# Loading w1 of the later experts as four transfers of 32 rows each

## The chip, the core and the metric

The kernel runs on one core of a Trainium2 chip. The metric is the device time of one execution in microseconds; the time before is 1105.34 us, the median of three runs (1098.51 to 1108.52).

## The reference

Windowed attention (8 batches, 8 heads, 576 positions, head size 64; half the heads plain, half dilated) feeds a mixture of experts over its 4608 rows of 512:

```python
top2 = np.argpartition(-noisy_logits, 2, axis=1)[:, :2]
...
for e in range(E):                              # E = 8
    for k in range(2):
        mask = top2[:, k] == e
        h = np.maximum(x[mask] @ w1[e], 0.0)    # w1[e]: 512 x 1024
        out[mask] += top2_w[mask, k, None] * (h @ w2[e])   # w2[e]: 1024 x 512
```

All is float32.

## The kernel before

The program has two stages. Up to about 240 us it computes attention and the gate, writes the attention's rows to a scratch tensor in DRAM (`xs`) and a table of (row, weight) entries per expert (`tab`). From then on it works through the eight experts. Expert 0 is fixed; the order of the other seven is found at run time, so their weights are read at an address that is held in a register (`EID`, `row`, lines 681 to 687).

An expert's tokens are at most 1152 to 1216, in three blocks of 3, 4 and 2 or 3 tiles of 128 tokens. For a block, `up` (line 811) runs 8 x 12 matmuls into PSUM buffers named `up`, and for each of the eight f ScalarE (ACT) takes the relu into `hh` (line 827) and VectorE (DVE) the rest into `hl` (line 829). `down` (line 877) then runs 24 matmuls per tile into one of two PSUM buffers named `dn` (line 865); DVE scales the result into `y` (line 874) and GpSimd (POOL) scatters it with an add into the output (line 842). Each float32 operand is held as a high and a low part, and three products of parts replace one product.

w1 of an expert comes in four chunks `kc` of 128 rows x 1024, 512 KB each. `stage_w1` (line 692) has SyncE (SP) issue the load into a buffer `ws`, and `split_w1` (line 699) has ACT cast it into `w1h` (line 703) and DVE subtract into `w1l` (line 705). The pool of `ws` has two buffers, shared with the loads of w2 (line 709). So the loads of chunks 2 and 3 are issued only when DVE has taken chunks 0 and 1, which it does after the last `up` of the expert before. Meanwhile PE runs four tiles of `down`, and then needs the new w1.

In the later experts the rows of a chunk are not contiguous in DRAM. The tokens' rows are gathered in pieces of 128 columns and transposed in blocks of 32 x 32, so that partition 32 q + d of chunk c stands for column 128 q + 32 c + d. The load of chunk kc therefore takes four blocks of 32 rows, 128 rows apart, one for each quadrant q of the partitions.

Each engine executes its own instructions in the order of the program. That order is made by a list of due times (`plan` and `tick`, lines 893 to 904) that is kept in units of PE's work; it decides between which matmuls a load, cast or gather is written. The order on SP's queue is the order of issue: the index loads of a later expert (lines 744, 747, 749: `ixt`, `ixs`) and the loads of w2 stand behind the loads of w1.

Of the kernel before, what the change touches and what calls it, by code (L numbers as in the profile page):

```python
# [46 lines left out]
def attention_moe_kernel(ctx, tc, qt, kp, kd, vpl, vdl, w_gate, w_noise, noise, w1, w2, out, CAPS=(1216, 1216, 1216, 1184, 1184, 1152, 1152, 1152), SPLITS=(0, 384, 896)):  # L47
    nc = tc.nc
    tensor, vector, scalar, gpsimd, sync = nc.tensor, nc.vector, nc.scalar, nc.gpsimd, nc.sync
# [636 lines left out]
    def row(w, e):  # L686
        return w[e] if isinstance(e, int) else w[bass.ds(e, 1)].rearrange("o a b -> (o a) b")
# [4 lines left out]
    def stage_w1(e, kc):  # L692

        s = late["stage"].tile([128, FF], F32, name="ws", tag="ws")
        sync.dma_start(s, w1[0][128 * kc:128 * kc + 128] if type(e) is int else
                       row(w1, e).rearrange("(q c d) f -> c q d f", q=4, c=4)[kc])
        ST[1, kc] = s

    def split_w1(kc):
# [292 lines left out]
    for kc in range(4):  # L992
        a, b = ((-3, 2), (-2, 3), (4, 6), (5, 7))[kc]
        at(L0 + SL_W1 + a, lambda kc=kc: stage_w1(0, kc))
        at(L0 + SL_W1 + b, lambda kc=kc: late.__setitem__(("w", kc), split_w1(kc)))
        at(L0 + SL_W1 + b + 1, lambda kc=kc: late.pop(("w", kc))())
# [78 lines left out]
    for e in range(E):  # L1075
# [50 lines left out]
        if not last:  # L1126
            t = start + (42 if first else 20)
            plan(t, lambda e=e: (new_idx(e + 1), idx_dma(e + 1, 0, CAPS[e + 1])))
            t = max(t + (14 if first else 9), at_[0, 1])
            plan(t - 0.5, lambda e=e: idx_copy(e + 1, 0, CAPS[e + 1]))  # L1130
            plan_x(e + 1, 0, t, *((6, 13) if first else (9, LAG)))
            plan_x(e + 1, 1, t + (18 if first else 27), *((6, 12) if first else (9, LAG)))
            t = at_[0, 2] + dur(e, 2, False)
            plan(t - 8, lambda e=e: (stage_w1(EID[e + 1], 0), stage_w1(EID[e + 1], 1)))
            for c in range(4):
                plan(t + 0.5 + 3 * c, lambda c=c: split_w1(c), 1.2)
                if c < 2:
                    plan(t + 0.6 + 3 * c, lambda c=c, e=e: stage_w1(EID[e + 1], c + 2))
# [15 lines left out]
    with tc.If(big > 0):  # L1154
        with tc.For_i(0, E, 1) as r:
            e = nc.values_load(ci[0:1, bass.ds(r, 1)], min_val=0, max_val=E - 1)
# [74 lines left out]
```

## Time and profile before

| | |
|---|---|
| runs | 1098.51, 1105.34, 1108.52 us |
| the profiled execution | 1100.93 us |
| its span, first to last instruction | 1099.3 us |
| mean granted TensorE clock | 0.962 |
| busy: PE, POOL, DVE, ACT | 93%, 48%, 42%, 29% of the span |
| loads of w1 and w2 on SP's queue (`ws`) | 64, 512 KB each |
| mean DMA rate over the span | 121 GB/s |

PE is the TensorE matmul queue, PEld its weight loads. A row "ACT w1h L703 <- DMA ws<-in_moe_w: 109.7, 13, 11.2" reads: ACT stood idle before the instructions of line 703 that write w1h until a DMA that writes ws had landed, 109.7 us in all, 13 times, 11.2 us the longest. Times in the timeline count from the first instruction. A granted clock of 1.00 is TensorE's full clock.

### The profile page before, as it was taken

Reading aid. Unit: us, or ns where it says so; the run is one execution under the profiler, and the core shown is the slowest. Engines: PE = TensorE matmul, PEld = TensorE weight load, DVE = VectorE, ACT = ScalarE, POOL = GpSimd, SP = SyncE. Lnnn points to the kernel's source line nnn. Section 1 sums busy time; section 2 is a strip of 40 time slices with the busy share of each in tenths; the row PEclk is TensorE's granted clock in tenths of the full one; section 3 lists DMA queues with packets and bytes.
Section 4 is the critical chain, followed back from the end, with each engine's and each line's share of the span. In section 5 each row is a group of like instructions: output and inputs, shape, how many; then the busy total and the mean of one; then the engine's idle time right before and its main releaser. Section 6 shows DMA issues by size and latency. Waiting matters only on the chain. (4 is left out here: it accounts for less than half of the span.)

```text
span 1099.3 us, 18395 instructions
## 1 busy us (share of the span) xinstructions
PE 1020.7 (93%) x7274; PEld 856.7 (78%) x7275; DVE 463.2 (42%) x1060; ACT 318.2 (29%) x609; POOL 528.2 (48%) x727
## 2 busy tenths in 40 slices
PE   7997767679999999999999999999999999999996
PEld 4774645567787889978987889788878888888885
DVE  7673636545133544344344333433453334333221
ACT  6673535531112322232223122312231222222110
POOL 7004243555767455655544554465445555653112
PEclk9997988889999999999999999999999999999998
DMA  8899587465235243443444334334333533353123
GB/s 282 309 336 296 151 276 259 150 198 145 47 88 122 74 98 61 118 89 82 79 95 84 89 78 97 88 79 86 79 94 71 124 50 107 64 127 60 32 29 46
DMA packets 77530, 132.91 MB, mean 121 GB/s; under 512 B 29968, under 2 KB 39616, under 8 KB 76160
## 3 DMA queue, kind: packets, MB, share of 16 engines
q1 hardware_dynamic: 55088, 92.55, 26.5%
q0 software_dynamic: 22352, 39.15, 19.9%
q8 instruction: 58, 0.95, 0.4%
q14 instruction: 32, 0.26, 0.1%
HBM read 92.11 MB, written 39.54 MB: 120 GB/s over the span
## 5 line engine op out<-in xcount | busy, mean ns | idle before, releaser
L823 PE MATMUL up<-x,w1h 128*128 128x512 f32 (+4 forms) x1536 | 398.7, 345 | 12.4 <-DVE hl L829 7.8
L823 PEld LDWEIGHTS up<-x,w1h 128*128 128x128 f32 x1536 | 273.9, 190 | 41.0 <-DVE hl L829 9.4
L775 POOL DMA_INDIRECT g<-xs,ixi x258 | 265.2, 1028 | 84.2 <-issue 78.9
L823 PE MATMUL up<-x,w1l 128*128 128x384 f32 (+4 forms) x768 | 264.6, 344 | 0.8 <-DVE w1l L705 0.8
L865 PE MATMUL dn<-w2h,hh 128*128 128x512 f32 x576 | 227.2, 394 | 4.5 <-DVE y L874 3.6
L865 PE MATMUL dn<-w2h,hl 128*128 128x512 f32 x576 | 225.5, 392 | 1.8 <-issue 1.7
L865 PE MATMUL dn<-w2l,hh 128*128 128x512 f32 x576 | 225.4, 391 | 0.2 <-issue 0.2
L829 DVE SCALAR_TENSOR_TENSOR hl<-up,hh 128x384 fp32r<-128x384 f32 (+2 forms) x192 | 106.0, 556 | 231.0 <-ACT hh L827 176.7
L842 POOL DMA_INDIRECT out_rows<-y,ixs x67 | 107.4, 1603 | 189.8 <-DVE y L874 161.0
L827 ACT ACTIVATE hh<-up 128x384 fp32r<-128x384 f32 (+4 forms) x192 | 94.2, 498 | 264.1 <-PE up L823 205.7
L823 PEld LDWEIGHTS up<-x,w1l 128*128 128x128 f32 x768 | 145.9, 190 | 13.2 <-DVE w1l L705 1.4
L865 PEld LDWEIGHTS dn<-w2h,hh 128*128 128x128 f32 x576 | 108.9, 189 | 29.7 <-DVE y L874 5.9
L865 PEld LDWEIGHTS dn<-w2h,hl 128*128 128x128 f32 x576 | 108.8, 189 | 24.8 <-issue 1.8
L865 PEld LDWEIGHTS dn<-w2l,hh 128*128 128x128 f32 x576 | 109.0, 189 | 22.5 <-issue 0.6
L874 DVE TENSOR_SCALAR y<-dn,ixs 128x512 f32<-128x512 f32 x63 | 46.9, 748 | 145.1 <-PE dn L865 120.7
L794 ACT CAST x<-xr 128x512 fp32r<-128x512 f32 x67 | 40.5, 604 | 188.9 <-DVE xr L792 160.8
L628 POOL DMA_INDIRECT tab<-en,si x72 | 71.1, 988 | 34.8 <-issue 16.1
L705 DVE TENSOR_TENSOR w1l<-ws,w1h 128x1024 fp32r<-128x1024 f32 x32 | 38.8, 1219 | 96.0 <-ACT w1h L703 88.9
L306 POOL COPY spacer<-hh 1x1 f32<-1x1 f32 x72 | 24.2, 336 | 99.5 <-ACT hh L827 99.2
L703 ACT CAST w1h<-ws 128x1024 fp32r<-128x1024 f32 x32 | 33.0, 1047 | 117.8 <-DMA ws<-in_moe_w 109.7
L795 DVE TENSOR_TENSOR x<-xr,x 128x512 fp32r<-128x512 f32 x67 | 44.6, 666 | 18.0 <-ACT x L794 15.2
L792 DVE STREAM_TRANSPOSE xr<-g 128x512 f32<-128x512 f32 x67 | 45.7, 682 | 0.0
(186 smaller groups left out, 859.5 us busy)
## 6 DMA issues: line engine op xcount, KB each, us to landing
ws<-in_moe_w SPq DMA_DIRECT2D x64, 512.0 KB
out_rows<-zero SPq DMA_DIRECT2D x38, 256.0 KB
vd<-in_vdl SPq DMA_DIRECT2D x24, 390.0 KB
vp<-in_vpl SPq DMA_DIRECT2D x16, 585.0 KB
qt<-in_qt SPq DMA_DIRECT2D x14, 576.0 KB
xs<-x SPq DMA_DIRECT2D x24, 256.0 KB
kt<-in_kd SPq DMA_DIRECT2D x16, 320.0 KB
g<-xs,ixi POOLq DMA_INDIRECT x258
```

Source lines behind the costliest of these rows:

```text
L628: ins = gpsimd.indirect_dma_start(out=tab, out_offset=bass.IndirectOffsetOnAxis(ap=si[:, kq, t:t + 1], axis=0), in_=en[:, kq, t], in_offse ...
L705: return lambda: vector.tensor_tensor(b, s, a.bitcast(F32), op=OP.subtract)
L775: gpsimd.indirect_dma_start(out=g[:, j], out_offset=None, in_=xq, in_offset=bass.IndirectOffsetOnAxis(ap=IX[e][1][:, r0 // 32 + j:r0 // 32 ...
L792: vector.transpose(xr[:, :, 0:rn].rearrange("p c (g t) -> p g c t", t=32), g[:, 0:n].rearrange("p g (c d) -> p g c d", d=32))
L794: scalar.copy(xh[:, :, o:o + rn], xr[:, :, 0:rn])
L795: return lambda: vector.tensor_tensor(xl[:, :, o:o + rn], xr[:, :, 0:rn], xh[:, :, o:o + rn].bitcast(F32), op=OP.subtract)
L823: tensor.matmul(p[:, 0:n], lhsT=a[:, 128 * f:128 * f + 128], rhs=b[:, kc, 0:n], start=(i == 0), stop=(i == 11))
L827: scalar.activation(hh[:, f, 0:n], p[:, 0:n], AF.Relu)
L829: vector.scalar_tensor_tensor(hl[:, f, 0:m], p[:, 0:m], 0.0, hh[:, f, 0:m].bitcast(F32), op0=OP.max, op1=OP.subtract)
L842: ins = gpsimd.indirect_dma_start(out=out, out_offset=bass.IndirectOffsetOnAxis(ap=sc[0:rn, t, 1:2], axis=0), in_=y[0:rn], in_offset=None, ...
L865: tensor.matmul(p[0:rn], lhsT=a[:, f, o:o + rn], rhs=b[:, f % 2], start=(i == 0), stop=(i == 23))
L874: vector.tensor_scalar(y[0:rn], p[0:rn], wsc, None, op0=OP.mult)
```

## The change

Where the expert's number is only known at run time, the one transfer of 128 rows becomes four of 32 rows, one for each quadrant of the partitions. The same rows go to the same partitions. Expert 0 keeps its load of 128 contiguous rows.

```diff
     def stage_w1(e, kc):
 
         s = late["stage"].tile([128, FF], F32, name="ws", tag="ws")
-        sync.dma_start(s, w1[0][128 * kc:128 * kc + 128] if type(e) is int else
-                       row(w1, e).rearrange("(q c d) f -> c q d f", q=4, c=4)[kc])
+        if type(e) is int:
+            sync.dma_start(s, w1[0][128 * kc:128 * kc + 128])
+        else:
+            for q in range(4):
+                sync.dma_start(s[32 * q:32 * q + 32], row(w1, e)[128 * q + 32 * kc:128 * q + 32 * kc + 32])
         ST[1, kc] = s
```

Seven experts with four chunks each make 28 loads before and 112 transfers now. A loop at the end of the program, for experts with more tokens than planned, holds 4 loads more, which become 16; it is not entered with these inputs. The order of PE, ACT, DVE and POOL stays as it was; only SP has more instructions (525 rows where it had 333).

SP, the loads of chunks 2 and 3 of the fourth expert that runs, and the index loads behind them. `ws_5882` and `ws_5907` are the two buffers; DMAHW is a hardware DMA semaphore, of which there are eight in turn. Before:

```order
L695 DMA ws_5882<-in_moe_w1 128x1x1024 [waits DMAHW5_49,DMAHW3_49,DVE_49]
L695 ISA
L695 DMA ws_5907<-in_moe_w1 128x1x1024 [waits DMAHW6_49,DMAHW4_49,DVE_49]
L744 ISA
L744 DMA ixt_6197<-tab_58 32x37x2 [waits Pool_49]
L747 ISA
```

The same place now (each of the two loads has four transfers with an ISA row ahead of each; rows that repeat are left out):

```order
L699 DMA ws_5912<-in_moe_w1 32x1024 [waits DMAHW5_49,DMAHW4_49,DMAHW6_49,DMAHW3_49,DVE_49]
L699 ISA
L699 DMA ws_5912<-in_moe_w1 32x1024
...
L699 DMA ws_5940<-in_moe_w1 32x1024 [waits DMAHW2_49,DMAHW1_49,DMAHW7_49,DMAHW0_49,DVE_49]
...
L747 ISA
L747 DMA ixt_6233<-tab_58 32x37x2 [waits DMAHW3_49,Pool_49]
L750 ISA
```

The first transfer of each load waits for DVE and for the four transfers that filled the buffer last; the other three wait for nothing more. The index load that stood behind two issues stands behind eight.

ACT, the casts of that expert's w1. Before:

```order
L703 CAST w1h1_5904<-ws_5800 128x1024 [waits DMAHW4_49]
L703 CAST w1h2_5940<-ws_5882 128x1024 [waits DMAHW5_49]
L703 CAST w1h3_5956<-ws_5907 128x1024 [waits DMAHW6_49]
L794 CAST x_5670<-xr_5966 128x4x128 [waits DVE_49]
L794 CAST x_5670<-xr_6022 128x4x128 [waits DVE_49]
L827 ACTIVATE hh_6032<-up_6034 128x384 [waits PE_49,Activation_49,Pool_49]
```

Now:

```order
L706 CAST w1h1_5937<-ws_5827 128x1024 [waits DMAHW2_49,DMAHW7_49,DMAHW1_49,DMAHW0_49]
L706 CAST w1h2_5976<-ws_5912 128x1024 [waits DMAHW5_49,DMAHW6_49,DMAHW4_49,DMAHW3_49]
L706 CAST w1h3_5992<-ws_5940 128x1024 [waits DMAHW2_49,DMAHW7_49,DMAHW1_49,DMAHW0_49]
L797 CAST x_5694<-xr_6002 128x4x128 [waits DVE_49]
L797 CAST x_5694<-xr_6058 128x4x128 [waits DVE_49]
L830 ACTIVATE hh_6068<-up_6070 128x384 [waits PE_49,Activation_49,Pool_49]
```

Nothing has moved; a cast waits for four semaphores where it waited for one, and the casts of x and the relus of the next `up` stand behind it as before.

## The prediction

> **What bounds the kernel now.** I read the busy table first, then one window over the expert stage, then who waits for whom in it.
>
> ```profile
> PE 1020.7 (93%) x7274; PEld 856.7 (78%) x7275; DVE 463.2 (42%) x1060; ACT 318.2 (29%) x609; POOL 528.2 (48%) x727
> 300.00:1099.00 799.00, 779.18 (x3854) 669.64 (x3853) 305.09 (x491) 183.72 (x310) 403.72 (x501) 0.99 0.39 83
> ```
>
> The second row is the stretch in which all seven later experts run; its columns after the length are the busy times of PE, PEld, DVE, ACT and POOL, the granted clock, the share of the 16 DMA engines and GB/s. PE is busy 779.2 of 799 us. So whatever faster loads do for the other engines, the kernel gains only what PE loses by waiting. These are PE's waits in that stretch, all of them:
>
> ```profile
> PE dn L865 <- DVE y L874: 3.6, 3, 2.1
> PE up L823 <- DVE hl L829: 2.6, 4, 1.0
> PE dn L865 <- issue: 2.2, 3, 1.7
> PE up L823 <- ACT w1h L703: 1.6, 1, 1.6
> PE up L823 <- DVE w1l L705: 0.8, 2, 0.6
> PE up L823 <- issue: 0.5, 1, 0.5
> PE dn L859 <- DVE y L874: 0.4, 1, 0.4
> ```
>
> The columns are microseconds in total, how often, and the longest. The sum is 11.7 us. Only 2.4 us names w1 outright, so the question is what stands behind DVE's lateness in the rows on y and hl. The engines' own longest waits in the same stretch point at it:
>
> ```profile
> ACT w1h L703 <- DMA ws<-in_moe_w: 109.7, 13, 11.2
> DVE w1l L705 <- ACT w1h L703: 88.9, 17, 8.7
> ```
>
> Thirteen times ACT stands before a cast of w1 until its load lands, up to 11.2 us, and DVE stands behind ACT. One such place, the w1 load of the fourth expert that runs, in the timeline (start, length, engine, line, in brackets the idle time before and its cause):
>
> ```profile
> 538.16 2.35 SPq L695 DMA_DIRECT2D ws<-in_moe_w  x2
> ...
> 543.67 9.34 SPq L747 DMA_DIRECT2D ixs<-tab  x1
> ...
> 549.86 1.05 ACT L703 CAST w1h<-ws 128x1024 fp32r<-128x1024 f32 x1 [11.22 <-DMA ws<-in_moe_w]
> 556.45 1.05 ACT L703 CAST w1h<-ws 128x1024 fp32r<-128x1024 f32 x1 [5.54 <-DMA ws<-in_moe_w]
> ...
> 550.94 1.23 DVE L705 TENSOR_TENSOR w1l<-ws,w1h 128x1024 fp32r<-128x1024 f32 x1 [6.45 <-ACT w1h L703]
> 552.08 0.74 DVE L874 TENSOR_SCALAR y<-dn,ixs 128x512 f32<-128x512 f32 x1
> ...
> 552.88 0.50 PE L865 MATMUL dn<-w2h,hh 128*128 128x512 f32 x1 [1.20 <-DVE y L874]
> ```
>
> SP issues the loads of chunks 2 and 3 from 538.16 us on. Chunk 2 is cast 11.7 us later and chunk 3 18.3 us later. DVE takes its work in order, so y of a finished down tile (L874) waits behind w1l, and PE, which has two buffers for dn, stops 1.20 us. The DMA is the root, DVE passes it on, PE pays a little of it.
>
> Why is a load of 512 KB so slow? The queue shares in two windows, the first while only loads of w1 are on SP's queue, the second with two loads of w2 of the same size:
>
> ```profile
> q1 hardware_dynamic: 222, 0.89, 23.7%
> q1 hardware_dynamic: 544, 1.05, 64.2%
> ```
>
> The columns are packets, MB and share of 16 engines. In 10 us (499 to 509) w1 moves 0.89 MB at 23.7% of 16 engines, which is 3.8 engines: four work and twelve do nothing. In 5.4 us (489 to 494.4) w2 moves 1.05 MB on 10.3 engines on average. The source of the w1 load counts 4 blocks outermost, that of w2 does not.
>
> **The change part by part.** *The landing.* 28 loads become 112 transfers of 32 rows. No row shows a 128 KB transfer into 32 partitions, so I bound it. From above by today's rate, if the pieces stay on four engines: chunk 2 after 11.7 us and chunk 3 after 18.3 us, and nothing is won. From below by w2:
>
> ```profile
> 380.70 3.08 SPq L709 DMA_DIRECT2D ws<-in_moe_w  x2
> 384.71 1.05 ACT L716 CAST w2h<-ws 128x1024 fp32r<-128x1024 f32 x1 [3.29 <-DMA ws<-in_moe_w]
> ```
>
> A whole w2 load goes from issue to cast in 4.0 us. I take w2's figure, since the new pieces have a plain block of 32 rows on both sides, as w2 has plain rows, and no outer count of 4. *SP's issue* then comes first:
>
> ```profile
> L695 SPq DMA_DIRECT2D ws<-in_moe_w x28: 532/536/672, 300.1 to 959.6; - x28
> L709 SPq DMA_DIRECT2D ws<-in_moe_w x32: 372/373/3780, 223.7 to 1015.2; - x32
> L747 SPq DMA_DIRECT2D ixs<-tab x7: 373/9341/12181, 298.1 to 877.5; - x7
> ```
>
> The three numbers are the least, median and longest ns of one issue. Four issues at 0.37 to 0.54 us, each with some 0.1 us of register work, take 1.9 to 2.6 us. Chunk 2 can then be cast 2.6 + 4.0 = 6.6 us after the first issue at most, instead of 11.7, and chunk 3, whose issues queue behind, at about 2 x 2.6 + 4.0 = 9.2 us, instead of 18.3. With cast and subtraction (1.05 and 1.23 us) DVE is through with chunk 3 at 538.2 + 9.2 + 2.3 = 549.7 us. PE wants the next y at 551.7 us (552.88 less the wait of 1.20). So the cover is 2 us at the tightest place, and chunk 2, the one that delayed y there, is done by 547.1 us.
>
> *The stalls.* Of the 11.7 us I leave out both rows named "issue" (2.7 us) and 0.4 us of the hl row, which lies at 848 us, before any load of w1 for the next expert is waited for. The other three hl waits stand just behind w1 casts:
>
> ```profile
> PE up L823 <- DVE hl L829: 0.7, 1, 0.7
> PE up L823 <- DVE hl L829: 0.6, 1, 0.6
> PE up L823 <- DVE hl L829: 1.0, 1, 1.0
> PE up L823 <- DVE hl L829: 0.4, 1, 0.4
> ```
>
> The windows are 343 to 366, 650 to 672, 760 to 780 and 847 to 850 us. What goes is 11.7 - 2.7 - 0.4 = 8.6 us.
>
> *The clock.* Two of the stalls cost more than their length:
>
> ```profile
> 972.11 0.79 PE L865 MATMUL dn<-w2h,hh 128*128 128x512 f32 x1 [2.12 <-DVE y L874]
> ...
> 357.70:361.20 3.50, 3.50 (x11) 0.52 0.54 151
> 972.20:975.60 3.40, 3.40 (x9) 0.52 0.93 199
> ```
>
> After the 1.6 us and 0.6 us waits near 355 us, and after the one of 2.12 us that ends at 972.11, the granted clock falls to 0.52 for about 3.45 us (the last two rows give PE alone). Each loses 3.45 x 0.48 = 1.65 us, together 3.3 us. No other stall of w1's in this stretch is followed by a slow window. [...]
>
> *What costs nothing.* The other 84 issues take SP 84 x 0.64 = 54 us, 7.7 per expert, on a queue that now stands up to 12.2 us inside a single index load (L747, third number) right behind w1's packets. Each cast waits for four semaphores instead of one, on ACT, which is busy 184 of 799 us. Without that cover SP would delay the index loads by about 4 us (six more issues), and POOL the gathers behind them. POOL has room, since it stands waiting for ACT and so for PE's progress:
>
> ```profile
> POOL spacer L306 <- ACT hh L827: 99.2, 30, 5.6
> ```
>
> *Sum.* 8.6 + 3.3 = 11.9 us at most. I take off 0.9 us for small stalls that come back elsewhere: 11 us. The profiled execution took 1100.9 us (span 1099.3 and 1.6 around it), so it would take 1089.9. That execution lies 4.4 us under the median of the runs, 1105.3, from which I forecast 1105.3 - 11 = 1094.3 us, 1.0% less.
>
> **The rivals.** *Only half goes.* The three hl waits (2.3 us) come from x's own splits, not w1's, and the slow clock windows (3.3 us) fall on some other short stall. For it: no hl wait names w1. Against: all three lie within 10 us of a late cast. The gain is 11.9 - 2.3 - 3.3 = 6.3 us, the time 1099.
>
> *The pieces stay on four engines.* Then chunk 3 still needs 18.3 us and the change does nothing: 1105. For it: the rows do not show how engines are given out. Against: the loads behind the two queue rows have the same size and the same queue, and differ in the shape of the source. [...]
>
> *SP chokes: slower.* [...] If each of the eight pieces of chunks 2 and 3 held SP 3 us, the pair would be issued in 24 us and cast at 28 us, 9.7 us later than now. PE now starts the next expert's up pass just after the last w1l, so nearly all of that is a stall, seven times: 1105 + 7 x 9.7 = 1173. It decides from (18.3 - 4.0) / 8 = 1.8 us per issue. Against it: the long issues are the ones behind w1's backlog on four engines, which this change drains. [...]
>
> **How the numbers follow.** The forecast has a chance of 0.65, the half gain 0.19, no effect 0.09, choking 0.07. A measurement of this kernel can tell about 1% from no change, 11 us, which is where the forecast lies: I give it 0.40 of its 0.65 over that bound, as runs with longer stalls than the profiled one win more, and the half gain 0.04. So faster 0.44, same 0.25 + 0.15 + 0.09 = 0.49, slower 0.07. The range goes from the fastest run shown less the full gain and a bit (1098.5 - 11.9 - 1.6 = 1085) to the case without effect, 1106.
>
> **What would show it.** Right: ACT's wait for ws at w1h falls from 109.7 to under 30 us; the issue-to-cast time of chunk 2 from 11.7 to 4 to 7 us; L747's issue from 9.3 to under 1 us; PE's waits after 300 us from 11.7 to about 3 us, and no slow window after 300 us. Wrong: a w1 share on SP's queue still at 24%, issues of over 1.8 us at the new line, or PE waits that have moved to x, w2 or the gathers.

## The result and the profile after

| | before | after |
|---|---|---|
| median of the runs (4 each) | 1104.63 us | 1087.9 us |
| the profiled execution's span | 1099.3 us | 1086.8 us |
| ratio, 95% interval | | 0.9869 (0.9824 to 0.9914) |
| a second set of runs (13 and 6) | 1101.12 us | 1089.24 us |
| its ratio, 95% interval | | 0.9901 (0.9867 to 0.9936) |

The change is faster by 1.0 to 1.3%. The forecast was 1.0% and 1094.3 us. The ratios here and below are estimates from all runs with their intervals. They are not quotients of the medians, which are 0.985 and 0.989 here and elsewhere lie up to 0.0025 beside them.

PE's waits over the later experts, 300 us to the end, in the profile of the changed kernel; all of them (line 832 is the old 829, 830 the old 827):

```profile
PE xrp L792 <- issue: 2.7, 4, 1.1
PE up L826 <- DVE hl L832: 1.9, 1, 1.9
PE up L826 <- ACT hh L830: 0.8, 1, 0.8
PE up L826 <- issue: 0.5, 1, 0.5
```

No row names w1 or y any more. The transposes of line 792 belong to expert 0. The 1.9 us stand at 941.6 us, in an up pass that reads w1 loaded 100 us earlier, and I come back to them. The waits of ACT and DVE in the same stretch, which were 109.7 and 88.9 us:

```profile
ACT w1h L706 <- DMA ws<-in_moe_w: 39.1, 13, 5.8
...
DVE w1l L708 <- ACT w1h L706: 10.9, 9, 2.3
```

The same place as in the prediction, chunks 2 and 3 of the fourth expert, in the timeline of the changed kernel:

```profile
533.58 4.15 SPq L699 DMA_DIRECT2D ws<-in_moe_w  x8
...
539.21 0.37 SPq L750 DMA_DIRECT2D ixs<-tab  x1
...
539.85 1.05 ACT L706 CAST w1h<-ws 128x1024 fp32r<-128x1024 f32 x1 [5.83 <-DMA ws<-in_moe_w]
542.80 1.05 ACT L706 CAST w1h<-ws 128x1024 fp32r<-128x1024 f32 x1 [1.89 <-DMA ws<-in_moe_w]
...
542.08 0.75 DVE L877 TENSOR_SCALAR y<-dn,ixs 128x512 f32<-128x512 f32 x1
```

SP issues eight transfers in 4.15 us. Chunk 2 is cast 6.3 us after the first issue and chunk 3 after 9.2 us, where it was 11.7 and 18.3. The y that came at 552.08 and held PE for 1.2 us now runs at 542.08 and is done some 4 us before PE wants it. The index load (`ixs`) that held SP for 9.34 us takes 0.37 us.

SP's issue times in the changed kernel (least, median, longest ns of one), and SP's queue while nothing but w1's pieces are on it, 492 to 498 us:

```profile
L699 SPq DMA_DIRECT2D ws<-in_moe_w x112: 2/316/1276, 304.4 to 952.1; - x112
L750 SPq DMA_DIRECT2D ixs<-tab x7: 368/598/897, 302.5 to 856.9; - x7
...
q1 hardware_dynamic: 383, 1.04, 61.6%
```

Where w1 had 23.7% of 16 engines, it has 61.6%, the figure of w2's loads (64.2%). The median index issue went from 9.34 to 0.60 us.

### The profile page after: what moved, and what is told of

Its sections match the earlier page's. It is cut to its first block, busy times and chain, and to the rows that moved or that the text cites. A ratio compares the mean times of both kernels' runs of the same rounds, so it can differ in the third digit from the quotient of the medians.

```text
span 1086.8 us, 18768 instructions
## 1 busy us (share of the span) xinstructions
PE 1011.7 (93%) x7274; PEld 855.7 (79%) x7275; DVE 465.7 (43%) x1060; ACT 319.4 (29%) x609; POOL 534.5 (49%) x727
## 5 line engine op out<-in xcount | busy, mean ns | idle before, releaser
L826 PE MATMUL up<-x,w1h 128*128 128x512 f32 (+4 forms) x1536 | 396.7, 344 | 10.9 <-issue 8.2
L778 POOL DMA_INDIRECT g<-xs,ixi x258 | 269.7, 1045 | 84.0 <-issue 78.6
L306 POOL COPY spacer<-hh 1x1 f32<-1x1 f32 x72 | 26.4, 366 | 131.9 <-ACT hh L830 131.6
L371 PE MATMUL s<-kt,qt 128*32 128x128 f32 x1152 | 41.2, 288 | 9.9 <-DMA qt<-in_qt 5.4
L371 PEld LDWEIGHTS s<-kt,qt 128*32 128x32 f32 x1152 | 32.5, 115 | 20.3 <-issue 19.6
L708 DVE TENSOR_TENSOR w1l<-ws,w1h 128x1024 fp32r<-128x1024 f32 x32 | 38.8, 1218 | 20.8 <-ACT w1h L706 10.9
```

The lines of the kernel that those rows point to most:

```text
L371: tensor.matmul(s[32 * qd:32 * qd + 32, e], lhsT=QV[ty][:, b, x, 32 * ub:32 * ub + 32], rhs=KV[ty][:, :, b, x, 32 * ub:32 * ub + 64], star ...
L708: return lambda: vector.tensor_tensor(b, s, a.bitcast(F32), op=OP.subtract)
L778: gpsimd.indirect_dma_start(out=g[:, j], out_offset=None, in_=xq, in_offset=bass.IndirectOffsetOnAxis(ap=IX[e][1][:, r0 // 32 + j:r0 // 32 ...
L826: tensor.matmul(p[:, 0:n], lhsT=a[:, 128 * f:128 * f + 128], rhs=b[:, kc, 0:n], start=(i == 0), stop=(i == 11))
```

## The experiments

The theory: a load runs on as many engines as the outermost count of its source allows, four for the four blocks of rows; chunks 2 and 3 come late, ACT and DVE pass the lateness on in order, and PE pays with short stalls and slow clock windows. The rivals: that smaller pieces help whatever the engines; that w1's packets stand in the way of the gathers and scatters; that SP's own backlog is what costs.

To compare traces beyond the noise of the runs I cut PE's work into passes of `up` and `down` and took each pass's length from the timeline, from the first matmul of expert 0's last down pass to the first of the last down pass of all. Over twelve traces each pass has a shortest length that it reaches again and again to 0.05 us. "Excess" is what a trace has over the sum of these, 705.8 us. "At w1" is the part of it in the passes during which w1 is loaded and split or which use it first.

| kernel | ratio to before on its chip (95%) | excess | at w1 |
|---|---|---|---|
| before, first profile | | 18.6 us | 15.4 us |
| before, second profile | | 15.2 us | 10.9 us |
| the change, first profile | 0.9869 (0.9824 to 0.9914) | 3.4 us | 0.1 us |
| the change, second profile | 0.9901 (0.9867 to 0.9936) | 4.4 us | 1.2 us |
| one contiguous transfer | 0.9909 (0.9881 to 0.9937) | 0.1 us | 0.1 us |
| two transfers of 64 rows | 1.075 (1.0688 to 1.0812) | 87.1 us | 87.0 us |
| four transfers by columns | 0.9983 (0.9958 to 1.0008) | 11.0 us | 10.9 us |
| chunks 2 and 3 in quarters | 0.9915 (0.9891 to 0.9939) | 0.1 us | 0.1 us |
| the same, second set | 0.9928 (0.9898 to 0.9958) | 6.7 us | 0.9 us |
| chunks 0 and 1 in quarters | 1.0011 (0.9976 to 1.0046) | 14.3 us | 13.3 us |
| eight transfers of 16 rows | 0.9910 (0.9880 to 0.9940) | 0.1 us | 0.1 us |
| chunks 2 and 3 not loaded | 0.9891 (0.9852 to 0.9930) | 2.5 us | 0.1 us |

Part of "at w1" is not w1's in two rows. A slow clock window behind the stall at 940 to 957 us, which is not w1's (last section), reaches into the next pass: 1.4 of the 10.9 us of the second profile of before, and 1.1 of the 1.2 us of the second profile of the change.

The first four experiments ran on a chip where every kernel is faster, before too: 1036.01 us. What differs is the time up to expert 0's last down pass (274 to 277 us there, 327 to 339 us elsewhere), so only ratios are compared across sets.

Four expectations below asked for 14 us under before, give or take 4, or for 12 to 18; 14 us was the gain of the first set. The medians of those kernels lie 9.6, 8.8, 9.1 and 9.8 us under before, so all four missed on the low side. That they have the whole gain is read from the last column, not from the size. There may have been less to gain there: two kernels on these chips that still wait for w1 have 10.9 us (columns) and 13.3 us (chunks 0 and 1) at w1, where the first profile of before has 15.4.

### One transfer of contiguous rows

Where a diff below shows only a new load, it stands in place of the loop over q of the change.

```diff
-            for q in range(4):
-                sync.dma_start(s[32 * q:32 * q + 32], row(w1, e)[128 * q + 32 * kc:128 * q + 32 * kc + 32])
+            sync.dma_start(s, row(w1, e)[128 * kc:128 * kc + 128])
```

> The load of a chunk in one transfer of 128 rows that lie together in DRAM (so the rows of w1 are the wrong ones for the tokens' columns; all else is the same work). Theory: what counts is the outermost count of the source, 4 before, 128 here, so the transfer runs on 16 engines and the time is that of the change, 14 us under before, give or take 4; chunk 2 is cast 4 to 6 us after its issue. Rival (pieces): the gain comes from cutting the load into smaller transfers that share the queue better; not cut here, so no gain (within 4 us of before).

1026.39 us, 9.6 less than before's 1036.01. Over the stretch of the table PE has no wait at all, and SP's queue runs as with the quarters (536 to 541.5 us):

```profile
q1 hardware_dynamic: 287, 1.05, 62.3%
...
ACT w1h L705 <- DMA ws<-in_moe_w: 30.0, 12, 5.1
```

Not cutting the load brings the whole gain if the rows lie together. So pieces are not the cause, and the rival that they are falls.

### Two transfers of 64 rows

```diff
+            for h in range(2):
+                sync.dma_start(s[64 * h:64 * h + 64],
+                               row(w1, e).rearrange("(q c d) f -> c q d f", q=4, c=4)[kc, 2 * h:2 * h + 2])
```

> Two transfers of 64 rows, each of two blocks of 32 rows. Theory: outermost count 2, so two engines; the pair of chunks 2 and 3, 18.3 us on four engines, takes about 36 us, and each of seven experts stands 10 to 18 us: 60 to 125 us slower than before. Rival (pieces): half the cut, so between no effect and the change: 0 to 7 us faster.

1114.01 us, 78 more than before. SP's queue with w1 alone on it (509.5 to 517 us), the casts of one expert's chunks 2 and 3, issued from 505.72 us on, and PE's longest waits:

```profile
q1 hardware_dynamic: 79, 0.32, 10.7%
...
521.56 1.04 ACT L707 CAST w1h<-ws 128x1024 fp32r<-128x1024 f32 x1 [15.37 <-DMA ws<-in_moe_w]
533.00 1.05 ACT L707 CAST w1h<-ws 128x1024 fp32r<-128x1024 f32 x1 [10.39 <-DMA ws<-in_moe_w]
...
PE dn L869 <- DVE y L878: 40.8, 6, 8.7
PE dn L863 <- DVE y L878: 10.8, 1, 10.8
```

10.7% of 16 is 1.7 engines on average, under the two of the outermost count: nothing shows that the second transfer takes two others. The pair lands after 27 us and not the 36 I gave it, but the loss is inside the range, and it comes through y, as the theory has it.

### Four transfers by columns

```diff
+            for j in range(4):
+                sync.dma_start(s[:, 256 * j:256 * j + 256],
+                               row(w1, e).rearrange("(q c d) f -> c q d f", q=4, c=4)[kc, :, :, 256 * j:256 * j + 256])
```

> Four transfers per chunk, but cut by columns: each takes 256 of the 1024 columns of all 128 rows, so the outermost count stays 4. Theory: still four engines, no gain, and packets of 1 KB may make it slower: 0 to 25 us slower than before. Rival (pieces): as many and as large transfers as the change, so its gain, 10 to 18 us faster.

1035.31 us: no difference, as the theory says. As many transfers of the same size as in the change, and 21.2% of 16 engines (483 to 488 us):

```profile
q1 hardware_dynamic: 348, 0.35, 21.2%
...
ACT w1h L707 <- DMA ws<-in_moe_w: 107.3, 13, 11.2
...
L751 SPq DMA_DIRECT2D ixs<-tab x7: 373/2732/6380, 251.1 to 818.7; - x7
```

The last row has a median of 2.73 us where before has 9.34, but SP is not freed by it. The same place on SP in this kernel:

```profile
480.31 10.74 SPq L699 DMA_DIRECT2D ws<-in_moe_w  x8
...
496.64 2.07 SPq L753 DMA_DIRECT2D ixs<-tab  x1
```

The time has moved from the index load to the issues of w1: SP is through 18.4 us after the first issue, and before it was 18.0 us (553.24 + 2.92 - 538.16). So this kernel says nothing on the rival of SP's backlog. Against that rival stand the waits for what is queued behind w1, w2 and the index loads, after 300 us, first before and then after the change:

```profile
ACT w2h L716 <- DMA ws<-in_moe_w: 27.1, 13, 3.7
POOL ixi L754 <- DMA ixt<-tab: 8.7, 2, 6.1
```

```profile
ACT w2h L719 <- DMA ws<-in_moe_w: 29.1, 14, 4.0
POOL ixi L757 <- DMA ixt<-tab: 7.5, 2, 5.1
```

They did not fall by more than 1.2 us, and none of PE's waits before names w2 or a gather. A kernel that frees SP alone was not run.

### Only chunks 2 and 3, only chunks 0 and 1

```diff
         if type(e) is int:
             sync.dma_start(s, w1[0][128 * kc:128 * kc + 128])
+        elif kc < 2:
+            sync.dma_start(s, row(w1, e).rearrange("(q c d) f -> c q d f", q=4, c=4)[kc])
         else:
```

This is the first of two kernels; the second has `kc >= 2`.

> Only chunks 2 and 3 are loaded in quarters, chunks 0 and 1 as before. Theory: chunks 0 and 1 are issued some 40 us before they are cast and nobody waits for them, so the whole gain stays: 14 us under before, give or take 4, and ACT's wait for ws at w1h stays under 45 us. Rival (traffic): the gain comes from w1's packets leaving four engines that the gathers and scatters need as well; then about half of it, 5 to 8 us.

> Only chunks 0 and 1 are loaded in quarters, chunks 2 and 3 as before. Theory (lateness of chunks 2 and 3): no gain, within 4 us of before; ACT's wait for ws at w1h stays near 110 us. Rival (traffic on four engines): half the gain, 5 to 8 us.

Chunks 2 and 3 alone: 1027.19 us, 8.8 less, ratio 0.9915. Chunks 0 and 1 alone: 1094.52 against 1096.07 us, ratio 1.0011. ACT's wait in the first and the second:

```profile
ACT w1h L708 <- DMA ws<-in_moe_w: 36.6, 12, 5.7
```

```profile
ACT w1h L708 <- DMA ws<-in_moe_w: 115.1, 14, 11.4
...
PE dn L870 <- DVE y L879: 4.2, 2, 3.3
PE up L828 <- DVE hl L834: 3.3, 3, 2.2
```

The gain sits in chunks 2 and 3: the first kernel gains about as much as the contiguous transfer on the same chip (8.8 and 9.6 us) and has 0.1 us left at w1, the second keeps 13.3 us there. By its size alone 8.8 us would be as near to the rival's 5 to 8 us as to the theory's 10 to 18. The traffic of chunks 0 and 1 on four engines, with gathers beside it, costs nothing that can be measured, which is against the rival of the gathers.

### Eight transfers of 16 rows

```diff
+            for q in range(8):
+                r = 128 * (q // 2) + 32 * kc + 16 * (q % 2)
+                sync.dma_start(s[16 * q:16 * q + 16], row(w1, e)[r:r + 16])
```

> Eight transfers of 16 rows per chunk: still 16 engines by the theory, twice the issues on SP. At 0.5 us per issue chunk 3 is cast some 8 + 4 = 12 to 13 us after the first issue instead of 9.2. PE wants the second y 13.5 us after it, so the time is that of the change, 14 us under before, give or take 4. Rival (SP chokes): issues add up past the need, and most of the gain is lost, under 6 us.

1086.97 against 1096.07 us, 0.9910. Sixteen issues take SP 10.30 us, and chunk 3 is cast 14.0 us after the first:

```profile
534.47 10.30 SPq L700 DMA_DIRECT2D ws<-in_moe_w  x16
...
542.25 1.05 ACT L707 CAST w1h<-ws 128x1024 fp32r<-128x1024 f32 x1 [7.30 <-DMA ws<-in_moe_w]
548.46 1.05 ACT L707 CAST w1h<-ws 128x1024 fp32r<-128x1024 f32 x1 [5.16 <-DMA ixt<-tab]
```

That is later than the 12 to 13 us expected: an issue takes 0.64 us here with what stands between, where 0.5 was assumed. With pieces of 64 KB at that pace the queue is at 36.7% (493 to 502 us, only w1 on it), not at 62%:

```profile
q1 hardware_dynamic: 483, 1.00, 36.7%
```

PE still stands nowhere at w1. SP's extra issues are free up to this point, and choking, the slower rival of the prediction, does not begin at twice the issues.

### Chunks 2 and 3 not loaded

This diff is against the kernel before.

```diff
+        if type(e) is not int and kc >= 2:
+            ST[1, kc] = ST["kept", kc - 2]
+            return
...
+        ST["kept", kc] = s
```

> The kernel before without the loads of chunks 2 and 3 for the later experts: the casts take chunks 0 and 1 again, so half of w1 is wrong; all casts, subtractions and matmuls are there, and the two loads left stay single transfers. Theory: nobody waits for w1, so the gain is that of the change, 14 us, and this is the most that any faster load of w1 can bring: 12 to 18 us under before. Rival (traffic): the two loads left still hold four engines, 5 to 8 us.

1086.31 against 1096.07 us, 0.9891. Nothing is left at w1 (0.1 us) though chunks 0 and 1 still come on four engines. The change has 0.1 us left there too, so by the traces it has taken all that a faster load of w1 can bring.

### The change and the part of it once more

> The change once more, beside before on the same chip, for a narrower interval: by the sum of the stalls in the trace of before (8.6 us and two slow clock windows, 11.9) and what the trace of the change shows, 10 to 15 us faster, ratio 0.987 to 0.991.

> Only chunks 2 and 3 in quarters. Theory: nobody waits for chunks 0 and 1, so the same time as the change within 0.3%; with 56 issues fewer on SP it is not slower. Rival (traffic): some of the gain of the change is missing, 3 us or more.

> The kernel before, for a profile on this chip: after 300 us PE loses 8 to 15 us to waits, and up to three slow clock windows stand behind waits of 2 us and more; the span from the first up to the last down is 10 to 15 us longer than that of the change.

1089.24 us for the change and 1091.95 for chunks 2 and 3 alone, with before at 1101.12; by the medians the change is 11.9 us faster. The two versions differ by 2.7 us with overlapping intervals. In their traces the difference lies at 940 us, outside of what w1 touches (below), so the rival of the traffic has no support from it, but 2.7 us were not settled. In the second profile of before PE waits 12.3 us after 300 us, 2.9 of them in expert 0, and its passes are 15.2 us too long, 9.5 of them through w1. No slow window stands behind a w1 stall there: the loss comes in other portions from one execution to the next.

### Stalls made on purpose, and the clock

Here the changed kernel repeats one subtraction on DVE, so that PE has to wait for y.

```diff
+        reps = 1 + ([0, 3, 4, 5, 6, 7, 8, 9][calls[0]] if kc == 2 and calls[0] < 8 else 0)
+
+        def subtract():
+            for _ in range(reps):
+                vector.tensor_tensor(b, s, a.bitcast(F32), op=OP.subtract)
```

`calls[0]` counts the experts. The second kernel has a 6 for each of the seven.

> The changed kernel with DVE's subtraction of chunk 2 repeated 3, 4, 5, 6, 7, 8 and 9 times more in the seven later experts, 1.14 us each, so that PE is made to wait for y there by about 0, 0.5, 1.6, 2.7, 3.9, 5.0 and 6.2 us. What of the clock: by the two windows seen before, waits from about 2 us on are followed by a half-clock window of 3.4 us, so four or five windows after 300 us, and a loss of about 1.7 us each beyond the wait itself. [...] If the windows come from something else, they don't follow the waits.

> The changed kernel with the subtraction of chunk 2 repeated 6 times more in each of the seven experts, so that PE waits about 1.7 to 2.7 us each time. If the clock goes by how much of one window of its own, 3.4 us long and running freely, PE stood idle, then some of these like waits are followed by a slow window and others not: those with 2.1 us or more inside one window are, those cut by a window's edge are not. If it goes by the length of the wait, all or none are. [...]

Each ran once: 1114.21 and 1112.63 us. In the first the waits for y were 2.22, 1.75, 2.73, 4.11 and 7.55 us, from five repetitions on; a slow window stands behind those of 2.22, 2.73 and 4.11 us and none behind that of 1.75 (rows and table below). In the second they were 1.58 to 3.59 us.

The clock's record in the traces of before and of the change has two values, 1.00 and 0.50, and all changes between them lie on one grid of 3.413 us, to 0.002 us. For eleven of PE's waits over 1 us the table has how much of the wait lies in one window of the grid of its own trace, and whether the next window is slow ("dose" is the first kernel, "six each" the second):

| kernel, wait (start, us) | in one window, at most | next window slow |
|---|---|---|
| dose, 655.80, 1.75 | 1.75 | no |
| dose, 547.16, 2.22 | 2.22 | yes |
| dose, 762.38, 2.72 | 2.35 | yes |
| dose, 869.72, 4.11 | 3.28 | yes |
| six each, 447.84, 2.84 | 1.57 | no |
| six each, 556.80, 3.42 | 1.88 | yes |
| six each, 352.90, 3.59 | 2.95 | yes |
| six each, 878.18, 2.00 | 1.01 | no |
| six each, 962.24, 1.97 | 1.97 | yes |
| chunks 0 and 1, 961.05, 3.30 | 1.84 | no |
| before, 969.99, 2.12 | 2.07 | yes |

Rows of PE alone behind four of these, first the kernel with 3 to 9 repetitions, then that with six (length, busy, granted clock, DMA share, GB/s):

```profile
549.70:553.11 3.41, 3.41 (x9) 0.50 0.90 192
...
658.91:662.33 3.42, 3.42 (x17) 1.00 0.85 224
```

```profile
561.75:565.17 3.42, 3.42 (x10) 0.50 0.97 223
...
452.53:455.94 3.41, 3.41 (x17) 1.00 0.85 189
```

Nine or ten matmuls where there should be 17. A wait of 3.30 us had no slow window behind it and one of 1.97 us did; in the table it goes by the idle time within one window, with the border between 1.84 and 1.88 us of 3.41. A window need not be idle throughout: windows of 3.41 us with 1.88 to 3.28 us of idle time were followed by a slow one. The 2.1 us of the second expectation were too many, and a wait that a window's edge cuts (3.42 us at 556.80) can have a slow window behind it.

The profiles of before and of the change agree from 260 us on. Windows with one wait of 2.07 and 2.08 us (before, from 968.65 and from 268.92 us) were followed by a slow one, and a window with 1.68 us of one wait (the change, from 941.87 us) by a fast one. Where two waits share a window less sufficed once: 1.54 and 0.23 us, 1.77 together, were followed by a slow one (before, 296.22 to 299.64 us).

So in these runs the stalls make the slow windows, which supports the second term of the prediction, and whether a given stall does is a matter of where the grid falls.

## Why the prediction was right

**The bound.** PE's waits were the budget, and the experiments agree: the kernels in which nobody waits for w1 run the stretch at its floor, but for a stall that is not w1's, and gain no more than the change.

**The root.** 3.8 engines was read from the queue row, and the shape of the source as its cause was a choice between bounds. Counts of 4, 2 and 128 give 3.4 to 3.8, 1.7 and 10.0 engines (21.2 and 23.7, 10.7 and 62.3% of 16), whether the load is cut or not. A mean share does not count engines, and no record names the engine of a packet, but the packets on SP's queue say more. These are its totals in before, the change, the contiguous transfer, two transfers of 64 rows and eight of 16:

```profile
q1 hardware_dynamic: 55088, 92.55, 26.5%
q1 hardware_dynamic: 56768, 92.56, 27.6%
q1 hardware_dynamic: 55424, 92.55, 28.0%
q1 hardware_dynamic: 55088, 92.55, 25.2%
q1 hardware_dynamic: 58560, 92.56, 27.0%
```

The data is the same in all five; what differs is packets of 4 bytes (4208 in before, 5888 in the change). In the transfer records of before the two loads issued from 495.74 us on have four each (503.72 to 504.41 and 509.01 to 509.92 us), and in the change the eight pieces of 492 to 498 us have 128, 16 each. With 4 for a load of before, 2 for a transfer of 64 rows and 16 for every contiguous one, the change should have 112 x 16 - 28 x 4 = 1680 more than before, the contiguous one 28 x 16 - 28 x 4 = 336, two of 64 rows 56 x 2 - 28 x 4 = 0, and eight 224 x 16 - 28 x 4 = 3472. These are the differences to the packet. That each of them stands for one engine, so that a load before ran on 4 engines and pieces of 32 and of 16 rows on 16, is my reading. The transfers in flight on SP's queue fit it: from 499 to 509 us of before four packets were in flight 75% of the time, more than four 6% of it and never more than six; from 492 to 498 us of the change it was 8 to 16 for 70% of the time and more than 16 for 3%.

**The landing.** At most 6.6 and 9.2 us were worked out, 6.3 and 9.2 us measured. An issue was put at 0.37 to 0.54 us and took 0.32. That 9.2 was hit to the tenth is luck: eight issues took 4.15 us instead of 5.2, and chunk 3 was cast 5.1 us after the last of them instead of 4.0.

**The stalls.** Too small: 8.6 us and 3.3 us of clock, 11.9, against 15.4 us that the same trace of before shows at w1 by the lengths of the passes. The term that was mis-sized is the sum of idle times. A row of PE's waits counts from the modelled end of the matmul ahead, 0.16 us after the next could have started (0.39 us long at a pitch of 0.23). And the first matmul behind a stall takes 0.50 us instead of 0.39 and holds the next back by 0.11 us. So each stall costs about 0.3 us more than its row says: the pass with the wait of 1.20 us is 1.49 us too long, that with 0.62 us 0.91. A stall whose idle time is under 0.15 us has no row; the down pass at 427.9 us has none and is 0.4 us too long, that at 747.2 us the same. Ten rows at 0.3 us and these two passes make 3.8 us, about what is missing (3.5). The clock's 3.3 us were right for the execution that they were read from. That there were two slow windows in it is chance: the second profile of before has none behind a stall of w1.

**The deduction** of 0.9 us for stalls that come back elsewhere was not needed: 0.1 us is left at w1 in both profiles of the change.

**The sum.** 11 us were forecast. By the ratios the two sets measured 14.5 us (0.0131 x 1104.63) and 10.9 us (0.0099 x 1101.12), by the medians 16.7 and 11.9 us. The intervals of the two ratios overlap, so the runs do not show that the sets differ. The stalls of w1 do vary between executions: 15.4 and 9.5 us in the two profiles of before. That the sum came out near is in part luck: stalls priced too low by 3.5 us, in an execution with more slow clock windows behind them than the other one.

**The signs.** ACT's wait for w1 was to fall under 30 us and fell to 39.1 (32.9 in the second profile), for which PE did not wait. No slow window was to be left after 300 us: one stands at 303.6 us, behind waits of expert 0, and the second profile has one more at 942 us. PE's waits were to be about 3 us and are 5.9, 2.7 of them in expert 0. The other two came: chunk 2 is cast after 6.3 us, and an index issue takes 0.60 us in the median.

**The hidden cost.** Right: 84 more issues cost PE nothing, nor did 196 more (eight transfers per chunk). SP was relieved too, from 9.3 to 0.6 us per index load; that this is worth nothing by itself is argued from the waits that did not change, not shown by a kernel.

**The rivals.** "Only half goes" fell: the three hl waits behind w1 casts are gone. "The pieces stay on four engines" holds for pieces cut by columns (21.2% of 16) and not for quarters of rows (61.6%). "SP chokes" gave an issue 3 us and decided from 1.8; the longest at the new line was 1.28 us. Pieces by columns, on four engines, reached 4.44 us.

## What to carry to other kernels

Look at the share of the 16 DMA engines while one load is alone on its queue: 24% was 3.8 engines here, and the outermost count of the source is the first suspect; loads with an outermost count of 32 or 128, in pieces or whole, had 62% (61.6 and 62.3%). Then ask whether anybody waits: the same cure was worth 1% on the loads that ACT stood waiting for and nothing on those issued 40 us ahead. Price a stall on PE by the length of its pass rather than by the idle column (0.3 us more per stall here), and look in the clock's record for what stands behind it: in the table above a wait with 1.88 us or more in one window was followed by a window of 3.41 us at a clock of 0.50, about 1.7 us lost.

## What the hardware showed beyond that

An issue took SP 0.53 to 0.55 us in the median for the transfers on four engines, 0.52 us on two, and 0.32 to 0.37 us on 16. Whether that goes by the engines or by the shape of the source, these runs do not tell apart. Behind w1's packets the index load of 128 rows held SP 9.3 us in the median and 12.2 us at most with w1 on four engines, 11.1 and 19.9 us on two, and 0.6 and 0.9 us after the change. What it waits for there is not in the trace.

The chip of the first four experiments came to the first matmul of `up` after 183 to 185 us, the others after 220 to 229, with the same instructions. The passes from expert 0's last `down` on have the same floor on both. The two stages' rows (length, then PE, PEld, DVE, ACT, POOL, clock, DMA share, GB/s), of the contiguous transfer there and of the change here:

```profile
0.00:182.00 182.00, 153.75 (x3120) 120.39 (x3121) 128.52 (x446) 120.52 (x272) 76.70 (x144) 0.96 0.91 313
```

```profile
0.00:225.00 225.00, 172.92 (x3124) 130.22 (x3125) 128.72 (x446) 120.70 (x273) 75.59 (x144) 0.89 0.76 254
```

DVE and ACT do the same work, and the bytes are the same 57 MB (length times rate) in less or more time; the DMA engines are busy a smaller share of the longer stage, and the clock is lower where PE waits more. What makes the one chip slower in this stage is open.

A stall of about 2 us at 940 us (`up` waiting for hl, line 832) is in five of the eight profiles of the slower chips that have no added subtractions, before and after (1.93, 1.94, 1.95, 1.91, 2.67 us), and in none of the faster one. It is not w1's: it is there with chunks 2 and 3 not loaded (1.91 us) and with the change. Its cause is open.
